# Cluster attention and two mixers on one core: the set-up of the first two head pairs in another order

## The chip, the cores and the metric

The kernel runs on one core of one Trainium2 chip. The metric is the device time of one execution in microseconds; lower is better. Engines: PE (TensorE, matmuls and transposes), PEld (its weight loads), DVE (VectorE), ACT (ScalarE), POOL (GpSimd) and SP (SyncE, which here only issues DMAs). Every time in this document is in microseconds unless it says otherwise.

## The reference

Attention over clusters: every query and key row is assigned to the nearest of 16 centroids of its head, and a query sees only the keys with its own assignment. Two mixers follow.

```python
batch, n_heads, seq, head_dim = (2, 8, 768, 64)   # 16 centroids per head
q_assign = np.argmax(np.einsum('bhsd,hcd->bhsc', q_n, c_n), axis=-1)
k_assign = np.argmax(np.einsum('bhsd,hcd->bhsc', k_n, c_n), axis=-1)
mask = q_assign[:, :, :, None] == k_assign[:, :, None, :]
scores = np.where(mask, scale * np.matmul(q, k.transpose(0, 1, 3, 2)), -1000000000.0)
...
x = np.matmul(attn, v)          # softmax of scores; then heads joined to 512 columns
u = x + (xt @ U @ V).transpose(0, 2, 1)
x = u + np.maximum(u @ w_ch1, 0.0) @ w_ch2
u = x + (np.maximum(xt @ w_tok1, 0.0) @ w_tok2).transpose(0, 2, 1)
return u + np.maximum(u @ w_ch1, 0.0) @ w_ch2
```

The weights, U and V arrive as 64-bit floats and are converted to 32 bits inside the kernel.

## The kernel before

The order of work is written out by hand; the framework only adds the waits. Two heads make a pair, and there are eight pairs. The attention of a pair is twelve tiles of 128 queries by 768 keys, so 96 tiles in all, n = 0 to 95 (the "thirteenth tile" has n = 12).

A matrix product of 32-bit precision is made of operands split into a rounded high part and the rest (low part). For each pair and each of its two halves `a` (one head each) a query stack `qS` and a key stack `kS` hold high and low parts in 128 partitions, with 16 rows of the cluster mask in between; there are two sets of stacks, used in turn by even and odd pairs. Rows of the other half come by copies from SBUF to SBUF (`cross`, two DMAs of 32 partitions each).

The work around the change:

- **Set-up of pair 0** (`setup`): the centroids are loaded (issued at 0.72) and q and k of the pair (k issued at 1.17), stacks are cleared, the centroids are normalised on DVE and transposed on PE into `zc`. For each half ACT rounds q and k (L435, L436), POOL takes the low part of k (L437), DVE that of q (L438). Then the argmax: `scores` (eight small matmuls), `scores_out` (DVE transpose out of PSUM), `arg0` to `arg4` and `mask_rows`, after which eight small DMAs bring the mask rows into the stacks (`stack(0, a, "mask", ...)`, half of them issued by ACT, half by SP).
- **Pair 1 in the set-up**: `load_pair(1)` on SP, ACT rounds (`q_hi`, `k_hi`), SP copies the high parts into set 1 (`stack(1, a, "hi", sp)`, eight DMAs), and `scores(1)`, `scores_out`, `q_lo`, `k_lo` and the copies of the low parts (six DMAs) stand behind the first two tiles' score matmuls `s_mm` and maxima `s_max`. One half of the high copies has 384 + 192 + 2 x 96 KB, one of the low copies 192 + 2 x 96 KB: 2304 KB in all.
- **Tiles**: `step(n)` issues tile n's transposes `t_mm` (six), the score matmuls and maximum of tile n + 2, the exponential `s_exp` of tile n + 1 on ACT, the copies `t_out` of the transposes out of PSUM, and from tile 6 on the products with v (`pv`). The score matmuls of tile n + 2 write the banks that the exponential of tile n reads. Lists attach other work to a tile: `mid` and `low` (PE), `acts` (ACT, ahead of the exponential) and `late` (at the end).
- In those lists: pair 1's argmax on tiles 0 to 5 and its mask DMAs on 6; `load_pair(2)` on 1; `load_uv` (three copies of V and one of U, 192 KB each) on 3; the load of v for pair 1 on 4; pair 2's scores on 9, its `q_hi` on 7 and `k_hi` on 9; U's first conversion step (ACT, L96) on 11.

Later pairs are prepared like pair 2, a few tiles ahead of their own.

Of the kernel before, what the change touches and what calls it, by code (L numbers as in the profile page):

```python
# [10 lines left out]
F32R = mybir.dt.float32r  # L11
# [4 lines left out]
ALU = mybir.AluOpType  # L16
AX = mybir.AxisListType

P = 128
# [5 lines left out]
def tile_cluster_attention__then__two_mixers(  # L25
# [58 lines left out]
    def sub(eng, o, a, b):  # L84
        eng.tensor_tensor(out=o, in0=a, in1=b, op=ALU.subtract)  # L85
# [93 lines left out]
    def load_pair(g, eng=sp):  # L179
        b, p = divmod(g, NPAIR)  # L180
        eng.dma_start(Rq, qT[b, p])
        eng.dma_start(Rk, kT[b, p])
# [7 lines left out]
    def scores(g):  # L190
        p = g % NPAIR
        held["sc"] = bk = ring()
        for qd in range(4):
            src = (Rq, Rk)[qd // 2]
            mm(ps[32 * qd : 32 * qd + 32, bk, 0:HS], zc[:, ts(p, 32)], src[:, ts(qd % 2, HS)], True, True)

    def scores_out():
        dve.transpose(out=am1, in_=ps[:, held["sc"], 0:HS])
# [32 lines left out]
    def mask_rows(eng):  # L231
        eng.tensor_scalar(out=om, in0=ohT, scalar1=msk[:, 0:1], scalar2=msk[:, 1:2], op0=ALU.add, op1=ALU.mult)

    def q_hi():
        rnd(act, Hq.bitcast(F32R), Rq, 0.125)

    def k_hi():
        rnd(act, Hk.bitcast(F32R), Rk)

    def q_lo(eng, o):  # L240
        eng.scalar_tensor_tensor(out=o.bitcast(F32R), in0=Rq, scalar=0.125, in1=Hq, op0=ALU.mult, op1=ALU.subtract)

    def k_lo(eng, o):
        sub(eng, o.bitcast(F32R), Rk, Hk)
# [5 lines left out]
    def cross(o, src, a, eng):  # L250
        m, x, _ = rows(a)
        for i in range(2):
            eng.dma_start(o[x, 1 - i, :], src[m.start + 32 * i : m.start + 32 * i + 32])

    def stack(g, a, what, eng, Lq=Rq, Lk=Rk):
        q, k = f32(qS[g % NST][a]), f32(kS[g % NST][a])
        m, _, y = rows(a)
        if what == "hi":
            eng.dma_start(q[m, :, :], Hq[m].unsqueeze(1).to_broadcast([64, 2, S]))
            eng.dma_start(k[m, 1, :], Hk[m])  # L260
            cross(k, Hk, a, eng)
        elif what == "lo":
            eng.dma_start(k[m, 0, :], Lk[m])
            cross(q, Lq, a, eng)
        else:
            e = eng if type(eng) is tuple else (eng, eng)
            for h in range(2):
                e[h].dma_start(q[y, 0, ts(h, HS)], om[32 * h + 16 * a : 32 * h + 16 * a + 16])
                e[1 - h].dma_start(k[y, 0, ts(h, HS)], om[64 + 32 * h + 16 * a : 80 + 32 * h + 16 * a])
# [113 lines left out]
        return [lambda: rnd(act, uh, o), lambda: sub(dve, ul, o, f32(uh))]  # L383


    def setup():
        with tc.tile_pool(name="tmp", bufs=1) as tmp:
            cc = tmp.tile([P, 2, D], F32, name="cc")
            tiny = tmp.tile([P, 1], F32, name="tiny")
            act.dma_start(cc[:, 0, :], cen)  # L390
            sp.dma_start(cc[:, 1, :], cen)
            sp.dma_start(Rq, qT[0, 0])
            act.dma_start(Rk, kT[0, 0])
            load_v(0)
            make_identity(nc, ident)
            dve.memset(zc, 0.0)
            for t in (qS, kS):
                for i in range(NST):
                    (dve, pool)[i].memset(f32(t[i][1])[32:64], 0.0)
            wi = tmp.tile([P, 16], F32, name="wi")  # L400
            pool.iota(wi, pattern=[[-1, 16]], base=16, channel_multiplier=0, allow_small_or_imprecise_dtypes=True)
            dve.memset(msk[0:64, 0:1], 0.0)
            dve.memset(msk[0:64, 1:2], 1.0)
            dve.memset(msk[64:128, 0:1], -1.0)
            dve.memset(msk[64:128, 1:2], BIG)


            sq = tmp.tile([P, D], F32, name="sq")
            n2 = tmp.tile([P, 1], F32, name="n2")
            n1 = tmp.tile([P, 1], F32, name="n1")  # L410
            nr = tmp.tile([P, 1], F32, name="nr")
            dve.tensor_tensor(out=sq, in0=cc[:, 0, :], in1=cc[:, 0, :], op=ALU.mult)
            dve.tensor_reduce(out=n2, in_=sq, axis=AX.X, op=ALU.add)
            dve.tensor_scalar(out=n2, in0=n2, scalar1=2.0 ** -100, scalar2=None, op0=ALU.max)
            act.activation(n1, n2, AF.Sqrt)
            dve.reciprocal(nr, n1)
            dve.tensor_tensor(out=nr, in0=nr, in1=n2, op=ALU.mult)
            dve.tensor_tensor(out=n1, in0=n1, in1=nr, op=ALU.add)
            dve.tensor_scalar(out=n1, in0=n1, scalar1=0.5, scalar2=1e-6, op0=ALU.mult, op1=ALU.add)
            dve.reciprocal(nr, n1)  # L420
            dve.tensor_scalar(out=cc, in0=cc, scalar1=nr, scalar2=None, op0=ALU.mult)
            ct = ps[:, 6, 0:P]
            pe.transpose(ct, cc.rearrange("p a d -> p (a d)"), ident)
            for a in range(2):
                dve.tensor_copy(
                    zc[64 * a : 64 * a + 64, :].rearrange("p (h j) -> p h j", j=32)[:, :, 16 * a : 16 * a + 16],
                    ct[64 * a : 64 * a + 64].rearrange("p (h j) -> p h j", j=32)[:, :, 16 * a : 16 * a + 16],
                )
            dve.tensor_copy(wcl, wi)

            l = p32[0]
            for a in range(2):
                m, _, _ = rows(a)
                q, k = qS[0][a], kS[0][a]
                rnd(act, q[m], Rq[m].unsqueeze(1).to_broadcast([64, 2, S]), 0.125)  # L435
                rnd(act, k[m, 1, :], Rk[m])  # L436
                sub(pool, k[m, 0, :], Rk[m], f32(k[m, 1, :]))  # L437
                dve.scalar_tensor_tensor(out=l[m].bitcast(F32R), in0=Rq[m], scalar=0.125, in1=f32(q[m, 0, :]), op0=ALU.mult, op1=ALU.subtract)  # L438
                cross(f32(k), f32(k[:, 1, :]), a, (act, sp)[a])
                cross(f32(q), l, a, sp)  # L440
            act.activation(tiny, n1, AF.Exp, scale=0.0)
            scores(0)
            scores_out()
            load_pair(1)
            arg0()
            arg1(dve)
            arg2()
            arg3(dve)
            arg4()
            mask_rows(dve)  # L450
            for a in range(2):
                stack(0, a, "mask", (act, sp))
            q_hi()
            k_hi()
            for a in range(2):
                stack(1, a, "hi", sp)
            s_mm(0)
            s_mm(1)
            s_max(0)
            s_max(1)  # L460
            scores(1)
            scores_out()
            q_lo(dve, Rq)
            k_lo(pool, Rk)
            for a in range(2):
                stack(1, a, "lo", sp)


    x_ = xn[:, 1].rearrange("p a b c -> p (a b c)")
# [97 lines left out]
    def at(d, s, f):  # L567
        d.setdefault(max(s, 0), []).append(f)

    for g in range(G):  # L570
        s0 = NTT * g
        for h in range(2):
            s = s0 + 2 * NT * h + 4 * NT + 1
            at(mid, s, lambda q=2 * g + h: merge(q))
            at(late, s, lambda q=2 * g + h: merge_out(q))
        n, s1 = g + 1, s0
        if 2 <= n < G:
            at(late, s1 - 8 if n > 2 else 1, lambda g=n: load_pair(g))
            at(low, s1 - 3, lambda g=n: scores(g))
            at(acts, s1 - 5, q_hi)  # L580
            at(acts, s1 - 3, k_hi)
            for s, f in ((-3, scores_out), (-2, arg0), (-1, lambda: q_lo(dve, Rq)),
                         (-1, lambda: arg1(pool)), (-1, lambda: k_lo(pool, Rk)), (3, arg2), (3, lambda: arg3(pool)),
                         (5, arg4), (5, lambda: mask_rows(pool))):
                at(late, s1 + s, f)
            for what, s in (("hi", -2), ("lo", 1), ("mask", 7)):
                for a in range(2):
                    at(late, s1 + s, lambda g=n, a=a, w=what: stack(g, a, w, sp))
        if n < G:
            at(late, s1 + 6 if n > 1 else 4, lambda g=n: load_v(g))  # L590
# [6 lines left out]
    for t in range(NS):  # L597
# [5 lines left out]

        at(mid, s, za)
        at(late, s if s == 69 else s + 1, lambda t=t: zadd_out(0, t, held["za"]))
    for s, f in ((0, arg0), (1, lambda: arg1(pool)), (2, arg2), (3, lambda: arg3(pool)), (4, arg4), (5, lambda: mask_rows(pool))):
        at(late, s, f)
    for a in range(2):
        at(late, 6, lambda a=a: stack(1, a, "mask", sp))
    at(late, 3, load_uv)  # L610
    for i, s0, ss in ((0, 11, (12, 12, 12, 12)), (1, 13, (14, 16, 18, 20))):
        at(acts, s0, uv[i][0])
        for f, s in zip(uv[i][1:], ss):
# [360 lines left out]
```

## Time and profile before

| | us |
|---|---|
| median of 3 runs | 767.53 (767.29 to 768.66) |
| the profiled execution | 767.95 |
| its span (first to last instruction) | 766.2 |
| PE busy | 738.7 (96%) |
| DVE busy | 467.1 (61%) |
| ACT busy | 310.1 (40%) |
| POOL busy | 166.4 (22%) |

The share of an engine is an average over stages with different limits. The 1.75 us between the profiled execution's time and its span lie ahead of the first and behind the last instruction. Times in the rows of the trace count from the start of the span.

### The profile page before, as it was taken

The numbers are of one execution on the slowest core, as the hardware profiler recorded it, in microseconds if no ns is written. First come the engines' busy times: TensorE is split into PE (matmuls) and PEld (weight loads), VectorE is DVE, ScalarE is ACT, GpSimd is POOL, SyncE is SP. The second block draws the span as 40 slices with busy tenths as digits, with TensorE's granted clock in tenths as the row PEclk, the third lists the DMA queues.
The fourth block names the chain that finished last, engine by engine and source line by source line (L and its number), as shares of the span: only waits on it lengthen the run. The fifth ranks groups of instructions, "written<-read, shape, count | busy, mean of one in ns | idle before, by whom it ended". The sixth has DMA issues, their size and how long they took to land.

```text
span 766.2 us, 10466 instructions
## 1 busy us (share of the span) xinstructions
PE 738.7 (96%) x3845; PEld 582.1 (76%) x3845; DVE 467.1 (61%) x689; ACT 310.1 (40%) x565; POOL 166.4 (22%) x147
## 2 busy tenths in 40 slices
PE   1899999999999999999999999999999999999998
PEld 0667766766666688888888888888888888888886
DVE  6778988877777366875758587666675432122113
ACT  3777877867776343332232324323232311111010
POOL 3321432421310122321322122125211410000000
PEclk9999999999999999999999999999999999999999
DMA  5886777875311344753632699967885647555652
GB/s 152 191 185 185 179 186 188 243 183 134 87 63 55 112 165 151 287 193 138 220 131 89 222 346 368 337 238 259 283 286 215 214 144 274 192 192 195 243 192 83
DMA packets 51714, 149.38 MB, mean 195 GB/s; under 512 B 7792, under 2 KB 15984, under 8 KB 49616
## 3 DMA queue, kind: packets, MB, share of 16 engines
q1 hardware_dynamic: 51152, 148.01, 59.7%
q10 hardware_dynamic: 512, 0.72, 0.3%
q8 instruction: 30, 0.49, 0.3%
q14 instruction: 20, 0.16, 0.1%
HBM read 97.32 MB, written 32.51 MB: 169 GB/s over the span
## 4 chain that ended last, share of the span: by engine, by line
PE 92%; DVE 3%; DMA 2%; ACT 2%; issue 1%; SPq 0%; ACTq 0%; DVEq 0%
PE ps L73 82%; PE ps L314 7%; DVE nm L292 1%; DMA xn<-in_U_dram 1%; ACT p L297 1%; ACT qk L78 1%; PE ps L377 1%; PE ps L822 1%; PE ps L334 1%; DMA sq__81<-in_qT_dram 1%; DMA qk<-om 0%; SPq L476 0%; DVE u_sb L100 0%; DVE xn L373 0%; DVE qk L85 0%
## 5 line engine op out<-in xcount | busy, mean ns | idle before, releaser
L727 DVE SCALAR_TENSOR_TENSOR gl<-ps,gh 128x512 fp32r<-128x512 f32 x84 | 58.0, 691 | 209.6 <-ACT gh L726 209.6
L73 PE MATMUL ps<-gh,qk 128*128 128x512 f32 x544 | 179.6, 391 | 0.1
L726 ACT ACTIVATE gh<-ps 128x512 fp32r<-128x512 f32 x84 | 50.2, 598 | 312.9 <-PE ps L73 311.5
L73 PE MATMUL ps<-qk 112*128 112x384 f32 (+2 forms) x456 | 110.8, 370 | 13.0 <-DMA qk<-om 10.3
L73 PEld LDWEIGHTS ps<-gh,qk 128*128 128x128 f32 x544 | 102.1, 188 | 21.6 <-issue 0.5
L292 DVE TENSOR_REDUCE nm<-ps 128x1 f32<-128x768 f32 x96 | 91.8, 956 | 41.5 <-PE ps L73 38.8
L73 PEld LDWEIGHTS ps<-qk 112*128 112x128 f32 (+1 forms) x456 | 77.2, 192 | 44.5 <-issue 20.7
L73 PE MATMUL ps<-gl,qk 128*128 128x512 f32 x272 | 106.1, 390 | 0.0
L85 POOL TENSOR_TENSOR qk<-c__77,qk 128x512 fp32r<-128x512 f32 x40 | 54.9, 1381 | 197.0 <-ACT qk L78 169.1
L297 ACT ACTIVATE p<-ps,nm 128x768 f32<-128x768 f32 x96 | 86.6, 902 | 7.4 <-DVE nm L292 6.8
L314 PE MATMUL ps<-ident,p 128*128 128x128 f32 x576 | 82.1, 275 | 2.6 <-DVE z L360 0.6
L314 PEld LDWEIGHTS ps<-ident,p 128*128 128x128 f32 x576 | 67.6, 140 | 12.8 <-ACT p L297 2.6
L73 PE MATMUL ps<-u2h,qk 128*128 128x512 f32 x224 | 73.9, 391 | 0.0
L73 PE MATMUL ps<-pt,vr 128*64 128x384 f32 x384 | 72.1, 498 | 0.0
L321 ACT COPY pt<-ps 128x512 f32<-128x512 f32 x96 | 56.1, 584 | 35.1 <-PE ps L314 34.7
L73 PEld LDWEIGHTS ps<-gl,qk 128*128 128x128 f32 x272 | 51.1, 188 | 10.2
L73 PE MATMUL ps<-u1h,qk 128*128 128x512 f32 x160 | 52.6, 390 | 0.0
L100 DVE TENSOR_SCALAR c__77<-c__77 128x512 f32<-128x512 f32 (+2 forms) x47 | 49.1, 1045 | 0.8 <-ACT c__77 L96 0.7
L73 PEld LDWEIGHTS ps<-u2h,qk 128*128 128x128 f32 x224 | 42.1, 188 | 8.6
L109 DVE SCALAR_TENSOR_TENSOR c__77<-c__76,c__77 128x512 int32<-128x512 int32 (+2 forms) x47 | 43.4, 923 | 1.5
L106 DVE SCALAR_TENSOR_TENSOR c__77<-c__76,c__77 128x512 int32<-128x512 int32 (+2 forms) x47 | 43.5, 925 | 1.1
L73 PE MATMUL ps<-u2l,qk 128*128 128x512 f32 x112 | 43.6, 390 | 0.0
(146 smaller groups left out, 1017.0 us busy)
## 6 DMA issues: line engine op xcount, KB each, us to landing
qk<-scr_b SPq DMA_DIRECT2D x72, 512.0 KB, 4.2
c__76<-in_wa_dram SPq DMA_DIRECT2D x16, 1024.0 KB, 4.8
qk<-scr_a SPq DMA_DIRECT2D x32, 512.0 KB, 7.6
c__76<-in_wb_dram SPq DMA_DIRECT2D x24, 512.0 KB, 5.1
scr_b<-qk SPq DMA_DIRECT2D x24, 512.0 KB, 4.2
scr_a<-wx SPq DMA_DIRECT2D x16, 512.0 KB, 2.9
scr_a<-qk SPq DMA_DIRECT2D x16, 512.0 KB, 2.7
qk<-sq__81 SPq DMA_DIRECT2D x14, 384.0 KB, 4.0
```

The lines of the kernel that those rows point to most:

```text
L73: pe.matmul(o, lhsT=l, rhs=r, start=start, stop=stop, **kw)
L78: act.activation(o, i, AF.Copy, scale=scale)
L85: eng.tensor_tensor(out=o, in0=a, in1=b, op=ALU.subtract)
L100: dve.tensor_scalar(out=dst, in0=dst, scalar1=2.0 ** -15, scalar2=122879.9921875, op0=ALU.max, op1=ALU.min)
L106: dve.scalar_tensor_tensor(out=d, in0=lo, scalar=29, in1=d, op0=ALU.logical_shift_right, op1=ALU.bitwise_or)
L109: dve.scalar_tensor_tensor(out=d, in0=hi, scalar=-0x40000000, in1=d, op0=ALU.bitwise_and, op1=ALU.bitwise_or)
L292: dve.tensor_reduce(out=nm[:, n % 4 : n % 4 + 1], in_=ps[:, b0 : b0 + 2, 0:HS], axis=AX.XY, op=ALU.max, negate=True)
L297: act.activation(p32[n % NP32].rearrange("p (j k) -> p j k", j=2), ps[:, b0 : b0 + 2, 0:HS], AF.Exp, bias=nm[:, n % 4 : n % 4 + 1], accum_ ...
L314: pe.transpose(ps[:, tb[j], ts(i, P)], p32[n % NP32][:, ts(c, P)], ident)
L321: act.copy(o, ps[:, tb[j], :])
L726: act.activation(gh, o, AF.Relu)
L727: dve.scalar_tensor_tensor(out=gl, in0=o, scalar=0.0, in1=f32(gh), op0=ALU.max, op1=ALU.subtract)
```

## The change

In the set-up, all four clearings of stacks go to POOL. Pair 0's argmax scores are issued after its first half's roundings; the low parts of both halves are taken in two small functions, `low_q` and `low_k`: the first half's ahead of the argmax (DVE and POOL), the second half's behind it (both on DVE). The key copies of the first half are issued by SP and those of the second by ACT (it was the other way round). PE is given 48 transposes of the identity into a bank that nobody reads, ahead of the first tile's matmuls. Pair 1 leaves the set-up but for its load, which GpSimd's queue issues behind the second half's low parts. Its scores, rounding (k on POOL), low parts, argmax and copies are attached to tiles 1 to 6; two steps of its argmax (`arg3`, `mask_rows`) go from POOL to DVE. `load_pair(2)` goes from tile 1 to 4, pair 2's `q_hi` from tile 7 to 9, and `load_uv` from tile 3 to the end of tile 6.

```diff
--- before.py
+++ after.py
@@ -383,6 +383,8 @@
         return [lambda: rnd(act, uh, o), lambda: sub(dve, ul, o, f32(uh))]
 
 
+    WARM = 48
+
     def setup():
         with tc.tile_pool(name="tmp", bufs=1) as tmp:
             cc = tmp.tile([P, 2, D], F32, name="cc")
@@ -394,9 +396,9 @@
             load_v(0)
             make_identity(nc, ident)
             dve.memset(zc, 0.0)
-            for t in (qS, kS):
-                for i in range(NST):
-                    (dve, pool)[i].memset(f32(t[i][1])[32:64], 0.0)
+            for i in range(NST):
+                for t in (qS, kS):
+                    pool.memset(f32(t[i][1])[32:64], 0.0)
             wi = tmp.tile([P, 16], F32, name="wi")
             pool.iota(wi, pattern=[[-1, 16]], base=16, channel_multiplier=0, allow_small_or_imprecise_dtypes=True)
             dve.memset(msk[0:64, 0:1], 0.0)
@@ -428,20 +430,31 @@
                 )
             dve.tensor_copy(wcl, wi)
 
-            l = p32[0]
+            l = p32[3]
+
+            def low_q(a):
+                m, _, _ = rows(a)
+                dve.scalar_tensor_tensor(out=l[m].bitcast(F32R), in0=Rq[m], scalar=0.125, in1=f32(qS[0][a][m, 0, :]), op0=ALU.mult, op1=ALU.subtract)
+                cross(f32(qS[0][a]), l, a, sp)
+
+            def low_k(a, eng):
+                m, _, _ = rows(a)
+                sub(eng, kS[0][a][m, 0, :], Rk[m], f32(kS[0][a][m, 1, :]))
+
             for a in range(2):
                 m, _, _ = rows(a)
                 q, k = qS[0][a], kS[0][a]
                 rnd(act, q[m], Rq[m].unsqueeze(1).to_broadcast([64, 2, S]), 0.125)
                 rnd(act, k[m, 1, :], Rk[m])
-                sub(pool, k[m, 0, :], Rk[m], f32(k[m, 1, :]))
-                dve.scalar_tensor_tensor(out=l[m].bitcast(F32R), in0=Rq[m], scalar=0.125, in1=f32(q[m, 0, :]), op0=ALU.mult, op1=ALU.subtract)
-                cross(f32(k), f32(k[:, 1, :]), a, (act, sp)[a])
-                cross(f32(q), l, a, sp)
+                cross(f32(k), f32(k[:, 1, :]), a, (sp, act)[a])
+                if a == 0:
+                    scores(0)
+            low_q(0)
+            low_k(0, pool)
             act.activation(tiny, n1, AF.Exp, scale=0.0)
-            scores(0)
             scores_out()
-            load_pair(1)
+            for i in range(WARM):
+                pe.transpose(ps[:, 5, ts(i % 4, P)], ident, ident)
             arg0()
             arg1(dve)
             arg2()
@@ -450,20 +463,13 @@
             mask_rows(dve)
             for a in range(2):
                 stack(0, a, "mask", (act, sp))
-            q_hi()
-            k_hi()
-            for a in range(2):
-                stack(1, a, "hi", sp)
+            low_q(1)
+            low_k(1, dve)
+            load_pair(1, pool)
             s_mm(0)
             s_mm(1)
             s_max(0)
             s_max(1)
-            scores(1)
-            scores_out()
-            q_lo(dve, Rq)
-            k_lo(pool, Rk)
-            for a in range(2):
-                stack(1, a, "lo", sp)
 
 
     x_ = xn[:, 1].rearrange("p a b c -> p (a b c)")
@@ -575,9 +581,9 @@
             at(late, s, lambda q=2 * g + h: merge_out(q))
         n, s1 = g + 1, s0
         if 2 <= n < G:
-            at(late, s1 - 8 if n > 2 else 1, lambda g=n: load_pair(g))
+            at(late, s1 - 8 if n > 2 else 4, lambda g=n: load_pair(g))
             at(low, s1 - 3, lambda g=n: scores(g))
-            at(acts, s1 - 5, q_hi)
+            at(acts, s1 - 5 if n > 2 else 9, q_hi)
             at(acts, s1 - 3, k_hi)
             for s, f in ((-3, scores_out), (-2, arg0), (-1, lambda: q_lo(dve, Rq)),
                          (-1, lambda: arg1(pool)), (-1, lambda: k_lo(pool, Rk)), (3, arg2), (3, lambda: arg3(pool)),
@@ -603,11 +609,14 @@
 
         at(mid, s, za)
         at(late, s if s == 69 else s + 1, lambda t=t: zadd_out(0, t, held["za"]))
-    for s, f in ((0, arg0), (1, lambda: arg1(pool)), (2, arg2), (3, lambda: arg3(pool)), (4, arg4), (5, lambda: mask_rows(pool))):
+    at(low, 1, lambda: scores(1))
+    for s, f in ((1, scores_out), (1, q_hi), (1, lambda: rnd(pool, Hk.bitcast(F32R), Rk)), (2, lambda: k_lo(pool, Rk)), (2, arg0),
+                 (2, lambda: arg1(pool)), (3, lambda: q_lo(dve, Rq)), (5, arg2), (5, lambda: arg3(dve)), (6, arg4), (6, lambda: mask_rows(dve))):
         at(late, s, f)
-    for a in range(2):
-        at(late, 6, lambda a=a: stack(1, a, "mask", sp))
-    at(late, 3, load_uv)
+    for what, s in (("hi", 2), ("lo", 3), ("mask", 6)):
+        for a in range(2):
+            at(late, s, lambda a=a, w=what: stack(1, a, w, sp))
+    at(late, 6, load_uv)
     for i, s0, ss in ((0, 11, (12, 12, 12, 12)), (1, 13, (14, 16, 18, 20))):
         at(acts, s0, uv[i][0])
         for f, s in zip(uv[i][1:], ss):
```

## Rows read from the trace of the kernel before

**Rows 1.** Waits of PE from 45 to 766: total, times, longest.

```profile
PE ps L377 <- DVE xn L342: 0.7, 1, 0.7
```

**Rows 2.** Timeline from 31.8 to 62: start, duration, engine, line, operation, [idle before].

```profile
45.53 0.95 PE L73 MATMUL ps<-qk 112*128 112x384 f32 x4 [0.55 <-DMA qk<-om]
...
47.44 0.38 ACT L96 ACTIVATE u_sb<-xn 128x192 f32<-128x192 f32 x1
...
47.73 0.88 ACT L297 ACTIVATE p<-ps,nm 128x768 f32<-128x768 f32 x1
...
49.89 0.98 PE L73 MATMUL ps<-qk 112*128 112x384 f32 x4
```

**Rows 3.** Timeline from 0 to 32, PE.

```profile
7.83 0.85 PE L73 MATMUL ps<-sq__81,zc 128*32 128x384 f32 x2 [0.55 <-DVE zc L425]
...
19.03 2.90 PE L73 MATMUL ps<-qk 112*128 112x384 f32 x8 [9.70 <-DMA qk<-om]
...
23.98 1.04 PE L314 MATMUL ps<-ident,p 128*128 128x128 f32 x8
...
28.12 0.98 PE L73 MATMUL ps<-qk 128*128 128x384 f32 x4 [1.98 <-ACT p L297]
```

**Rows 4.** Timeline from 0 to 32, DVE, ACT and POOL.

```profile
1.34 1.34 DVE L399 MEMSET qk<- 32x1536 f32 x1 [0.35 <-issue]
...
4.53 0.23 DVE L412 TENSOR_TENSOR sq<-cc 128x64 f32<-128x64 f32 x1
...
5.86 1.48 ACT L78 ACTIVATE qk<-sq__81 64x1536 fp32r<-64x1536 f32 x1 [0.42 <-DMA sq__81<-in_qT_dram]
...
8.16 2.34 POOL L85 TENSOR_TENSOR qk<-sk__82,qk 64x768 fp32r<-64x768 f32 x1 [3.90 <-ACT qk L78]
...
10.91 0.95 DVE L438 SCALAR_TENSOR_TENSOR p<-sq__81,qk 64x768 fp32r<-64x768 f32 x1 [2.08 <-ACT qk L78]
11.63 1.28 ACT L441 ACT_TABLE_LOAD   x1
...
11.90 0.58 DVE L198 STREAM_TRANSPOSE am<-ps 128x384 f32<-128x384 f32 x1
...
13.10 0.87 DVE L215 TENSOR_TENSOR am<-am,amx 128x384 bf16<-128x384 f32 x1
...
16.19 0.48 DVE L232 TENSOR_SCALAR om<-ohT,msk 128x384 f32<-128x384 bf16 x1
...
26.10 0.94 DVE L292 TENSOR_REDUCE nm<-ps 128x1 f32<-128x768 f32 x1
...
27.08 0.90 ACT L297 ACTIVATE p<-ps,nm 128x768 f32<-128x768 f32 x1 [1.88 <-DVE nm L292]
```

**Rows 5.** Chain of waits from 14 to 60: start, duration, what.

```profile
37.16 6.62 DMA xn<-in_U_dram
...
43.80 1.75 DMA qk<-om
```

**Rows 6.** DMA issues around 1, 14.78 and 34.21: KB, time to landing.

```profile
...
sk__82<-in_kT_dram ACTq DMA_DIRECT2D x1, 384.0 KB, 4.9
...
cc<-in_cen_dram ACTq DMA_DIRECT2D x1, 32.0 KB, 1.9
...
sk__82<-in_kT_dram SPq DMA_DIRECT2D x1, 384.0 KB, 3.6
...
sk__82<-in_kT_dram SPq DMA_DIRECT2D x1, 384.0 KB, 5.8
```

**Rows 7.** Timeline of SP's queue from 20 to 35.

```profile
20.32 0.70 SPq L259 DMA_DIRECT2D qk<-sq__81  x1
...
30.54 1.23 SPq L253 DMA_DIRECT2D qk<-sq__81  x2
33.71 0.33 SPq L181 DMA_DIRECT2D sq__81<-in_qT_dram  x1
...
34.60 1.60 SPq L476 DMA_DIRECT2D xn<-in_V_dram  x1
```

## The prediction

> **What bounds the kernel now.** I read the profile from the back to the front. The list of what PE waited for from 45 us to the end has six entries of one wait each, the longest 0.7 us, 3.0 us in all [rows 1]. So from about 45 us PE sets the end, and a change in the set-up is worth exactly what it moves the moment from which PE runs without a break. As the mark I take the fifteenth tile's score matmuls, now at 49.89 [rows 2]: from there on both programs issue the same PE work. What must be found is when the mark comes after the change.
>
> Before it PE starves twice. The first tile matmul starts at 19.03, after 9.7 us of waiting for the mask rows [rows 3]. The timeline shows what these waited for: DVE's subtraction for the second half (10.91) stands in front of the argmax, which runs from 11.90 to 16.67 [rows 4]. The second place is tile 12's matmuls at 45.53, released by a mask DMA [rows 2]; the chain of waits leads from it to the DMA of U, issued at 37.16 and landed at 43.78, with the mask DMA issued at 43.80 [rows 5]. I read from this that a DMA of SP is issued only when the one eight issues earlier has landed.
>
> **The change, part by part.**
>
> *Memsets.* Two of 1.34 us leave DVE [rows 4]. POOL does all four, from 1.35 to about 6.7, while it has nothing else until 8.16, so they cost nothing; without that cover they would hold POOL's subtraction. DVE's centroid arithmetic starts at 4.53 now [rows 4]; its data were issued at 0.72 and took 1.9 [rows 6], so it can start 1.9 sooner, and the argmax scores, now at 7.83 [rows 3], would be ready at 5.9. They then wait for k, issued at 1.17 and 4.9 in flight [rows 6]: 6.1. Two rounds of at most 0.85 end by 7.8.
>
> *The argmax first.* ACT has q's first half rounded at 5.86 + 1.48 = 7.34; DVE's first subtraction (0.95, as its twin) ends at 8.3 and the argmax follows at once, 3.6 us before its old 11.90. Its instructions took 16.67 - 11.90 = 4.77 [rows 4]. POOL's subtraction runs beside it to about 10.5 as now (8.16 + 2.34) and could hold the comparison (L215), due at 9.5, by up to 1.0; but L215 took 0.87 even now, longer than the steps around it, so something of that is in the 4.77 already, and I take nothing more. Mask rows: 13.1. ACT issues half of their DMAs; it runs its old instructions in another order, so it is through its table load at 11.63 + 1.28 = 12.9 [rows 4], just in time. The old 19.03 - 16.67 = 2.36 from rows to matmul [rows 3, 4] gives the first tile matmul at 15.45.
>
> *Unread transposes.* Rows show two paces of PE, though the clock column prints 1.00 throughout: eight score matmuls took 2.90 at 19.03 after 9.7 us without work, four took 0.98 at 28.12 after 1.98 us without [rows 3]; I read them as the 1.2 and the 2.4 GHz level. Eight transposes took 1.04 at 23.98 [rows 3]: at most 0.13 each at the fast pace, so 0.11 with the last one's tail taken off, and twice that, 0.22, at the slow. Forty-eight from 7.8 on end at 13.1 (all fast) or 18.4 (all slow). They are over by 15.45 if no more than 21 are slow. I take fewer, since by 23.98 PE was fast after 5 us of work, some of which was itself fast; then they cost nothing, and the first four matmuls take 0.98 instead of half of 2.90, 0.5 less. The first exponential starts at 15.45 + 0.98 + 0.94 for the maximum [rows 4]: 17.4.
>
> *Second pair by GpSimd's queue.* The load now waits for DVE's last two subtractions: 13.1 + 2 x 0.95 = 15.0. No DMA of GpSimd's queue is in this trace. By the nearest rows, k took 3.6 in the set-up and 5.8 later through SP [rows 6]; so it lands between 18.6 and 20.8. I take the middle, since both ends are the same transfer under different load. Its first readers are the scores in tile 1: exponentials at 17.4 and 18.4, the next matmuls 1.04 after the second (as 27.08 to 28.12 [rows 3, 4]), 0.98 for them and six transposes: 21.1; and ACT's rounding of q, behind the third exponential (20.4 to 21.3) and one copy out of PSUM (0.58, as L198): 21.9 to 22.8, priced as an exponential of the same shape, 0.90. So the load is hidden, with 0.3 to 2.5 to spare; a gain below nothing is excluded, since nothing reads it sooner. POOL's new rounding of k, priced as the nearest POOL row, 2.34 [rows 4], ends by 23.2. The Trainium skill (DMA: Bandwidth & Descriptors, Specifications) gives the GpSimd path about 1 us to the first byte and the others about 0.6; by that estimate the landing comes 0.4 later and is still hidden; no row here shows it.
>
> *The pair's copies on SP.* Fourteen DMAs, 2.3 MB by the code, are issued from 20.32 to 31.77 [rows 7], 0.2 MB a microsecond, back to back; that 11.45 stays. They start when q is rounded, at 22.8 and not 20.32: done 34.3. The third pair's load, now moved to tile 4, comes, as before, when the copies have landed, 33.71 - 20.32 = 13.4 after the first [rows 7] (the load of v fits in between): q at 36.2, k 0.5 later, landing 3.6 later [rows 6] at 40.3. Tile 9's scores read it; PE wants them at about 39, a new wait of 1.3. Eight mask DMAs follow on SP; the eighth waits for k, so it leaves SP at about 40.9. Then V, V, V and U, moved from tile 3 to behind the masks in tile 6. From the first V to U's landing it was 43.78 - 34.60 = 9.2 [rows 5, 7], with the 0.77 MB of q and k ahead of them; at 0.2 MB a microsecond that is 3.7, so 5.5 are left and U lands at 46.5. Bounds: 44.7, if only its and V's 0.77 MB count (3.8), and 50.1, if all 9.2 stay. I take 5.5 because q and k have landed by then.
>
> *The mark.* ACT's first step on U (0.38) stands in tile 11 ahead of the thirteenth exponential [rows 2]. Now U has been there for 3.7 us; after the change ACT waits for it: exponential at 46.9 (47.73 now), the mark 1.04 later: 47.95 instead of 49.89 [rows 2]. The 3.6 us won at the first tile, 4.1 with the faster matmuls, shrink to 1.9. Such a sum assumes that every other engine follows at once; DVE takes two argmax steps over from POOL in tiles 5 and 6 (about 1.0), and I leave 0.1 for it: 1.8. The profiled execution took 767.95, so 766.15; the median of the runs is 0.42 lower: 765.7.
>
> **Rivals.**
>
> *U is in time.* If V and U need only the 3.8, ACT waits no more than PE does. Then k is the last thing late: 40.3, rounding 0.90, an exponential to the next matmuls 1.04: tile 12's matmuls at 42.3 instead of 45.53, 3.2 won, 764.3. For it: their rings are empty by then. Against: U alone was 6.6 in flight [rows 5].
>
> *The gain is eaten at U.* If the third pair's k takes its present 5.8 instead of 3.6 [rows 6], mask, V and U come 2.2 later: mark at 50.15, 0.3 lost, 767.8: no change. For it: v's load now goes ahead of it. Against: V no longer runs beside it. A GpSimd load that lands after about 21.5 does the same, microsecond for microsecond.
>
> *The transposes hold PE, and slowly* (the other side). If all 48 run at 0.22, PE is at them until 18.4, the first tile comes 2.95 later and its matmuls at the slow pace another 0.5; everything up to U's landing follows: mark at 51.4, 1.5 lost, 769.0. It decides from the 22nd slow transpose. For it: no stretch of the trace has transposes alone, and matmuls after long idleness are slow. Against: at 23.98 eight transposes were fast, though right behind matmuls. The Trainium skill (TensorE: Matmul & The Clock Gate, Part 4: PE-mode transpose) says that transposes do not count as PE work in the way that raises the clock; by that rule this rival holds with its 769.0, and no row here refutes it.
>
> **How the numbers follow.** Forecast 0.48, U in time 0.12, gain eaten 0.20, slow transposes 0.20. The time is the forecast's, 765.7. On this kernel 0.2% is 1.5 us, about what a measurement can tell from no change. The forecast's own spread is 0.9 either way (k 0.7, U 0.6), so 0.33 of its 0.48 lies beyond 1.5; with U in time 0.45 is faster. Of the slow transposes 0.12, and 0.05 from U's far bound, are slower; 0.38 remain. The range runs from U in time to the slow transposes, 764.4 to 769.0; the forecast alone has 764.8 to 766.6.
>
> **What would show it.** The argmax from 8.3 to 13.1; first tile matmul at 15.45, its four within 1.0; transposes first 0.22 and then 0.11 apart, over by 15.4; GpSimd's loads landed by 20.8; first copy of the pair issued at 22.8; the third pair's k landed at 40.3; U landed at 46.5 and ACT waiting for it; the mark at 48.0. It is wrong if PE is still at transposes when the mask rows land, if tile 1's scores wait for GpSimd's load, if ACT finds U there, or if the copies take another time than 11.45.

## The result and the profile after

The changed kernel takes 771.72 us (median of 6 runs, 769.75 to 772.73) against 767.35 (766.90 to 768.66) for the kernel before, measured beside it: ratio 1.0052, 95% interval [1.0038, 1.0066]. It is slower by 4.4 us, where 1.8 faster was forecast, and outside the predicted range. The profiled execution took 772.73, the slowest of the six, with a span of 770.9 (766.2 before). Compared instruction by instruction on PE, it is 3.99 later at the mark (53.88 against 49.89) and 3.54 later at tile 18 (tiles are numbered from 0); it loses 0.4 near 260 us and 0.5 in small steps near 225 and 708; PE ends 4.49 later. So the start decides, as assumed, but with the other sign. The gain of the first tiles is real and lasts until tile 11, whose matmuls start 2.92 sooner than before (38.46 against 41.38); it is lost at tiles 12 to 14, which start 1.47, 2.90 and 3.99 later than before.

The timeline of PE after the change (columns as in [rows 2]):

```profile
7.98 7.17 PE L457 MATMUL ps<-ident 128*128 128x128 f32 x48
15.55 1.80 PE L73 MATMUL ps<-qk 112*128 112x384 f32 x8 [0.40 <-DMA qk<-om]
18.72 1.65 PE L73 MATMUL ps<-qk 112*128 112x384 f32 x4 [1.38 <-ACT p L297]
20.17 1.91 PE L314 MATMUL ps<-ident,p 128*128 128x128 f32 x8
21.90 1.62 PE L73 MATMUL ps<-qk 128*128 128x384 f32 x4
23.32 1.05 PE L314 MATMUL ps<-ident,p 128*128 128x128 f32 x4
...
38.46 0.95 PE L73 MATMUL ps<-qk 128*128 128x384 f32 x4
...
43.00 0.84 PE L73 MATMUL ps<-sq__81,zc 128*32 128x384 f32 x4 [1.70 <-DMA sq__81<-in_qT_dram]
45.01 0.89 PE L73 MATMUL ps<-sk__82,zc 128*32 128x384 f32 x4 [1.17 <-DMA sk__82<-in_kT_dram]
47.00 1.65 PE L73 MATMUL ps<-qk 112*128 112x384 f32 x4 [1.11 <-ACT p L297]
48.44 1.91 PE L314 MATMUL ps<-ident,p 128*128 128x128 f32 x8
50.01 1.63 PE L73 MATMUL ps<-qk 112*128 112x384 f32 x4
...
53.88 0.99 PE L73 MATMUL ps<-qk 112*128 112x384 f32 x4
```

The same tile 11 before:

```profile
41.38 0.94 PE L73 MATMUL ps<-qk 128*128 128x384 f32 x4
```

The first tile matmul comes at 15.55, 3.48 sooner than in [rows 3], and at the fast pace: eight in 1.80, where four took 0.98 and eight slow ones 2.90. The transposes are over at 15.15. Then four matmuls take 1.65 again, at 18.72 and at 47.00. The view of the busy time by stretch says why (start:end and length of the stretch, busy time of PE, PEld, DVE, ACT and POOL with the number of their instructions, granted clock of PE, share of the DMA engines, GB/s):

```profile
11.50:18.30 6.80, 5.45 (x41) 4.72 (x39) 5.07 (x8) 2.11 (x3) 1.30 (x2) 1.00 0.56 133
18.40:25.20 6.80, 6.48 (x28) 5.07 (x28) 2.62 (x4) 3.43 (x9) 0.83 (x1) 0.50 0.28 78
25.20:45.60 20.40, 16.64 (x108) 11.99 (x104) 13.76 (x19) 12.29 (x24) 4.81 (x4) 1.00 0.79 182
45.70:52.50 6.80, 5.69 (x24) 4.98 (x24) 2.76 (x4) 4.48 (x10) 2.08 (x3) 0.50 0.92 218
```

The granted clock is 0.50, the 1.2 GHz level, in two stretches, 18.4 to 25.2 and 45.7 to 52.5; they are called the first and the second dip below. The first begins at 18.36, inside the wait of 1.38 us ahead of 18.72. The second begins at 45.67, after waits of 1.70 and 1.17 us for the third pair's q and k; another of 1.11, for an exponential, follows ahead of 47.00. The profile of the kernel before has no such stretch: its first record of the clock is 1.0 at 22.97, and it stays there until the end of the work.

The dips are not the whole loss. Of the six runs of the changed kernel, the one with a mean granted clock of 1.000 took 769.75, still 2.4 more than the kernel before; the other five, at 0.990 to 0.996, took 771.00 to 772.73.

What PE and ACT waited for shows in the DMA issues between 13 and 52 (columns: KB of one, median us from issue to landing), and in the timelines of SP and ACT:

```profile
sq__81<-in_qT_dram POOLq DMA_DIRECT2D x1, 384.0 KB, 4.4
sk__82<-in_kT_dram POOLq DMA_DIRECT2D x1, 384.0 KB, 5.7
...
sk__82<-in_kT_dram SPq DMA_DIRECT2D x1, 384.0 KB, 5.3
...
qk<-p SPq DMA_DIRECT2D x2, 96.0 KB, 5.5
xn<-in_U_dram SPq DMA_DIRECT2D x1, 192.0 KB, 4.0
```

```profile
15.78 1.17 SPq L253 DMA_DIRECT2D qk<-p  x2
25.77 0.70 SPq L259 DMA_DIRECT2D qk<-sq__81  x1
...
39.26 0.35 SPq L181 DMA_DIRECT2D sq__81<-in_qT_dram  x1
39.71 0.37 SPq L182 DMA_DIRECT2D sk__82<-in_kT_dram  x1
...
44.98 0.51 SPq L269 DMA_DIRECT2D qk<-om  x1
45.53 1.52 SPq L482 DMA_DIRECT2D xn<-in_V_dram  x3
47.09 0.42 SPq L483 DMA_DIRECT2D xn<-in_U_dram  x1
```

```profile
24.41 0.59 ACT L321 COPY pt<-ps 128x512 f32<-128x512 f32 x1 [1.66 <-PE ps L314]
24.89 0.85 ACT L78 ACTIVATE sq__81<-sq__81 128x768 fp32r<-128x768 f32 x1
...
42.93 0.84 ACT L78 ACTIVATE sq__81<-sq__81 128x768 fp32r<-128x768 f32 x1 [4.04 <-DMA sq__81<-in_qT_dram]
...
51.12 0.39 ACT L96 ACTIVATE u_sb<-xn 128x192 f32<-128x192 f32 x1 [1.00 <-DMA xn<-in_U_dram]
51.41 0.88 ACT L297 ACTIVATE p<-ps,nm 128x768 f32<-128x768 f32 x1
```

They are to be read as one chain. The second pair's q is rounded at 24.89, behind a copy out of PSUM that waited for PE's transposes. The first copy of the pair follows at 25.77 (20.32 before, [rows 7]), and the third pair's load leaves 13.5 after it, at 39.26 (33.71 before). Its k lands at 39.71 + 5.25 = 44.96; the last mask DMA (44.98, eight issues behind that k), V (45.53) and U (47.09, landed 51.10) come behind it, and ACT waits 1.00 for U ahead of the exponential at 51.41. The mark is 2.47 behind that exponential; PE is at the low clock until 52.49 and comes to it late (1.02 behind it in e1, which has no second dip).

### The profile page after: what moved, and what is told of

Same layout as the page of the kernel before. It is cut to its first block, busy times and chain, and to the rows that moved or that the text cites. A ratio compares the mean times of both kernels' runs of the same rounds, so it can differ in the third digit from the quotient of the medians.

```text
span 770.9 us, 10567 instructions
## 1 busy us (share of the span) xinstructions
PE 750.2 (97%) x3893; PEld 592.4 (77%) x3893; DVE 464.2 (60%) x690; ACT 310.4 (40%) x564; POOL 167.2 (22%) x148
## 4 chain that ended last, share of the span: by engine, by line
PE 92%; DVE 3%; DMA 2%; ACT 2%; issue 1%; SPq 0%; DVEq 0%; ACTq 0%
PE ps L73 82%; PE ps L314 8%; DVE nm L292 1%; ACT p L297 1%; DMA qk<-om 1%; PE ps L377 1%; PE ps L334 1%; PE ps L831 1%; DMA sq__81<-in_qT_dram 1%; DMA qk<-scr_b 1%; ACT qk L78 1%; DVE xn L373 0%; DVE qk L85 0%; DVE amx L206 0%; DVE p L437 0%
## 5 line engine op out<-in xcount | busy, mean ns | idle before, releaser
L73 PE MATMUL ps<-qk 112*128 112x384 f32 (+2 forms) x456 | 112.4, 374 | 4.2 <-ACT p L297 3.2
L73 PEld LDWEIGHTS ps<-qk 112*128 112x128 f32 (+1 forms) x456 | 78.0, 194 | 35.1 <-ACT p L297 13.4
L314 PE MATMUL ps<-ident,p 128*128 128x128 f32 x576 | 84.0, 281 | 2.3 <-DVE z L360 0.6
L314 PEld LDWEIGHTS ps<-ident,p 128*128 128x128 f32 x576 | 70.0, 144 | 11.7 <-ACT p L297 2.4
L73 PEld LDWEIGHTS ps<-pt,vr 128*64 128x64 f32 x384 | 23.4, 136 | 26.5 <-issue 26.5
```

The source lines that it names most:

```text
L73: pe.matmul(o, lhsT=l, rhs=r, start=start, stop=stop, **kw)
L314: pe.transpose(ps[:, tb[j], ts(i, P)], p32[n % NP32][:, ts(c, P)], ident)
```

## The experiments

The theory after this result: the tiles from 12 on are set by a chain of one pair's load, its rounding, its 2.3 MB of copies, the next pair's load, and so on; the change starts that chain later by 5.4 us (first copy 25.77 against 20.32), and each wait of PE can bring the low clock on top. The rivals: GpSimd's queue alone, the unread transposes, U alone, or the argmax's new order. The mark is tile 14. The table has the times of one profile of each kernel, and the medians of its runs (us; the mark and tile 24 as differences from before's 49.89 and 73.85; the ratio is to the kernel before, measured beside it):

| kernel | first copy | third pair's k landed | U landed | mark | tile 24 | median | ratio, 95% interval |
|---|---|---|---|---|---|---|---|
| before | 20.32 | 40.04 | 43.78 | | | 767.35 | |
| after | 25.77 | 44.96 | 51.10 | +3.99 | +3.54 | 771.72 | 1.0052 [1.0038, 1.0066] |
| e1 | 25.92 | 44.88 | 50.94 | +2.38 | +2.86 | 770.48 | 1.0030 [1.0012, 1.0047] |
| e2 | 24.37 | 43.28 | 50.44 | +2.23 | +1.79 | 770.56 | 1.0026 [1.0012, 1.0041] |
| e3 | 25.22 | 44.39 | 50.53 | +2.73 | +3.39 | 771.83 | 1.0050 [1.0035, 1.0065] |
| e5 | 22.50 | 41.98 | 48.06 | -0.49 | -0.15 | 769.08 | 1.0015 [1.0000, 1.0029] |
| e6 | 22.83 | 41.95 | 48.90 | +0.33 | +0.09 | 769.05 | 1.0016 [1.0003, 1.0030] |
| e8 | 21.50 | 41.23 | 47.99 | -2.27 | +3.69 | 770.77 | 1.0035 [1.0016, 1.0054] |
| e9 | 21.52 | 40.36 | 48.09 | -3.12 | -1.06 | 768.51 | 1.0013 [0.9991, 1.0035] |
| e10 | 20.90 | 38.93 | 42.40 | -0.21 | -0.22 | 768.99 | 1.0018 [1.0009, 1.0027] |
| e11 | 21.14 | 40.79 | 49.85 | -2.70 | -2.62 | 765.19 | 0.9965 [0.9952, 0.9978] |
| e12 | 24.50 | 43.37 | 50.22 | +2.01 | +1.56 | 771.20 | 1.0037 [1.0024, 1.0050] |
| e4 | 24.57 | 43.06 | 49.80 | +1.18 | +1.18 | 770.95 | 1.0039 [1.0024, 1.0053] |

A profile is one execution, and the low clock comes in some executions of a kernel and not in others (above: 0.990 to 1.000 in runs of the changed kernel); so the place of a wait is read from the profile, and the price of a kernel from its median.

**e1: the second pair's load on SP.**

```diff
-            load_pair(1, pool)
+            load_pair(1)
```

> The changed kernel with pair 1 loaded by SP's queue at the same place of the program instead of by GpSimd's. Theory P (PE's slow stretch from 18.4 to 25.2 sets the time of q's rounding, and the copies on SP, the third pair's load and U follow it): the load lands up to 2 us sooner, but tile 1's scores and q's rounding still come at 24.3 to 24.9; the first copy of the pair stays within 0.5 us of 25.8 and the time within 0.5 us of the changed kernel's. Theory L (the GpSimd load, landed at 21.45, is the delay): the copies start 1.5 to 3 us sooner and the time falls by as much.

The load is issued 2.5 later (17.38) and lands in 3.3 and 3.5 at 20.66 and 21.61, no sooner than GpSimd's. The clock is at 0.5 from 18.62 to 25.45 all the same, and the first copy stays at 25.92. GpSimd's queue is not the cause by itself. The median falls by 1.2, more than the 0.5 expected: in this profile the clock doesn't fall a second time. U lands only 0.16 sooner than in the changed kernel (50.94), but the mark comes 1.02 behind the exponential instead of 2.47, and 1.60 sooner.

**e2: the clock kept up.** Twelve more unread transposes stand between the first two tiles' matmuls and the third's.

```diff
             s_mm(1)
+            for i in range(12):
+                pe.transpose(ps[:, 5, ts(i % 4, P)], ident, ident)
             s_max(0)
```

> The changed kernel with 12 more unread transposes behind the first two tiles' score matmuls, so that PE works through its idle time from 17.35 to 18.7. Theory P: if PE keeps the fast pace in tiles 0 and 1, q is rounded at about 22 and the copies start at 22.8 to 23.5 instead of 25.8, the third pair's k lands 2.5 to 3 us sooner, and the time falls by 2.5 to 4.5 us, back to that of the kernel before or a little under it. If the clock falls all the same, nothing changes and this run says nothing. Theory L: the copies start at 25 or later, less than 1 us won. Theory O (the order alone: pair 1's load and copies now start behind the argmax, whatever PE's pace): under 1 us.

The clock is 1.0 from 9.61 on, past the place of the first dip, and the first copy moves from 25.77 to 24.37: the first dip costs 1.4. The clock falls at 43.74 instead, after waits of 2.29 and 0.52 for the third pair's q and k. The first copy doesn't reach 22.8, so something else holds it, and the median falls by 1.2 and not by the 2.5 to 4.5 expected.

**e6: both together**, the lines of e1 and e2.

> The changed kernel with both: pair 1 loaded by SP's queue, and 12 more unread transposes behind the first two tiles' score matmuls. Each alone left the copies of pair 1 at 25.9 and 24.4. Theory R (two causes stand in parallel at tile 3: PE's slow pace, and the second half's q copies, which land at 21.2 to 21.7 because 768 KB of GpSimd's load go ahead of them in the rings): with both away tile 3's matmuls come at about 20.3 instead of 21.6 to 21.9, but k of pair 1 lands at 21.6, so the scores of tile 1 wait for it; copies start at 23.0 to 23.7, the mark (tile 14) at 51 to 52, the time 1 to 2 us under that of the changed kernel with the transposes alone. Theory P alone: nothing beyond what the transposes gave, copies at 24.4.

Now the first copy is at 22.83. The timeline of PE, and the DMA issues of the copies between the two halves:

```profile
18.45 0.98 PE L73 MATMUL ps<-qk 112*128 112x384 f32 x4
19.26 1.04 PE L314 MATMUL ps<-ident,p 128*128 128x128 f32 x8
20.05 0.95 PE L73 MATMUL ps<-qk 128*128 128x384 f32 x4
...
qk<-p SPq DMA_DIRECT2D x2, 96.0 KB, 2.2
```

The fourth tile's matmuls start at 20.05 instead of 21.90. They read the two 96 KB copies that cross q's low parts between halves (qk<-p). Behind GpSimd's 768 KB these were 5.5 in flight; ahead of the load, on SP, 2.2. In e12, whose front part is that of the changed kernel but whose profile has no dip there, PE names them:

```profile
18.43 0.98 PE L73 MATMUL ps<-qk 112*128 112x384 f32 x4 [1.37 <-ACT p L297]
19.25 1.04 PE L314 MATMUL ps<-ident,p 128*128 128x128 f32 x8
21.73 0.94 PE L73 MATMUL ps<-qk 128*128 128x384 f32 x4 [1.45 <-DMA qk<-p]
```

So either one alone hides the other: at the low clock the copies are in time, and at the high clock PE waits for them. Taken out together they are worth 2.94 at the first copy (1.40 and nothing alone). The median, 769.05, is 1.5 below e2's, as expected. What is left of e6's loss stands on ACT (timeline of e6): U is late by 3.06, and the mark is 1.02 behind the exponential.

```profile
48.92 0.37 ACT L96 ACTIVATE u_sb<-xn 128x192 f32<-128x192 f32 x1 [3.06 <-DMA xn<-in_U_dram]
49.20 0.88 ACT L297 ACTIVATE p<-ps,nm 128x768 f32<-128x768 f32 x1
```

**e3: no unread transposes.**

```diff
-    WARM = 48
+    WARM = 0
```

> The changed kernel without its 48 unread transposes. Theory P, as the rows of the kernel before read: PE starts its first tile at the slow pace at 15.5, is slow for the first two tiles as well, and the copies start within 1 us of 25.8; the time stays within 1 us of the changed kernel's, so the transposes bought nothing. Rival: the transposes are what made the clock fall at 18.4 (they were read as no work), and without them the clock rises at about 20 and the time falls by 2 us or more.

771.83 against 771.72: the 48 transposes neither gain nor cost anything that can be measured. They do bring the high clock sooner (first record 1.0 at 11.54; without them at 23.06) and make the first eight matmuls faster (1.80 against 2.90), but the tile after them starts only 0.21 sooner (18.72 against 18.93).

**e5: the second pair's roundings one tile sooner.**

```diff
-    for s, f in ((1, scores_out), (1, q_hi), (1, lambda: rnd(pool, Hk.bitcast(F32R), Rk)), (2, lambda: k_lo(pool, Rk)), (2, arg0),
+    for s, f in ((1, scores_out), (0, q_hi), (0, lambda: rnd(pool, Hk.bitcast(F32R), Rk)), (2, lambda: k_lo(pool, Rk)), (2, arg0),
-    for what, s in (("hi", 2), ("lo", 3), ("mask", 6)):
+    for what, s in (("hi", 1), ("lo", 3), ("mask", 6)):
```

> The changed kernel with q's and k's rounding of pair 1 attached to tile 0 instead of 1 and the high copies to tile 1 instead of 2; everything else is left. Theory C (the start of the copies on SP carries everything behind it): the first copy starts at about 22.0 to 22.6 instead of 25.8, all fourteen are out 3.2 to 3.8 us sooner, the third pair's k lands by as much sooner and the mark (tile 14's score matmuls, 53.88) comes 3 to 4 us sooner; time 767.5 to 768.5. Theory O2 (tiles 0 to 2 are late anyway, because PE is slow until 25.2): the copies start sooner, but tiles 3 to 8 keep their times and the mark moves by less than 1.5 us.

The first copy comes 3.27 sooner, U lands 3.04 sooner, and the mark is 4.48 sooner than in the changed kernel: 3.0 through U, the rest because the clock doesn't fall a second time. So the later start of the chain is the cause of most of the loss at the mark. The median falls by less than expected, to 769.08; a part of that in this profile is a wait of 1.6 for the DMA of a converted weight block (qk<-scr_b) near the end, which was 0.2 in the changed kernel's.

**e8 and e9: as e5, and U needed later; e9 with e2's transposes too.**

```diff
-    for i, s0, ss in ((0, 11, (12, 12, 12, 12)), (1, 13, (14, 16, 18, 20))):
+    for i, s0, ss in ((0, 15, (16, 16, 16, 16)), (1, 13, (14, 16, 18, 20))):
```

> Rounding and copies of pair 1 one tile sooner (as in the run before it), and U's conversion in tiles 15 and 16 instead of 11 and 12. With the rounding sooner alone, tile 12's matmuls came at 44.0, U landed at 48.06 and tile 14's matmuls at 49.40. Theory U (the wait for U is what stands between the two): tile 14 at 46.6 to 47.3, which is 2.6 to 3.2 before the kernel before; time 764.6 to 766. Rival (tile 14 is set by the maxima and by PE's products with v, not by U): tile 14 at 48.5 or later, under 1 us won.

> As the run before it with 12 more unread transposes behind the first two tiles' score matmuls. Theory R: rounding of q at 20.5 instead of 21.6, copies start at about 21.4, the third pair's k lands 1 us sooner, tile 14 about 1 us sooner than without them, 45.6 to 46.3; time 763.6 to 765. Rival (k's landing at 21.2 and its rounding by POOL at 22.0 hold the second copy, so the copies end when they did): within 0.4 us of the run without them.

The mark is 2.27 and 3.12 sooner than before the change: here the forecast's gain is, and more. But the medians, 770.77 and 768.51, lie far above the expected 764.6 to 766 and 763.6 to 765: the gain is lost again at tile 22. (The first copy comes at 21.52 in e9 and at 21.50 in e8, whose profile has no first dip even without the transposes.) In e9 ACT's list of waits from 60 to 70, and the DMA issues from 58 to 72, show the next link of the same chain, the fourth pair's load (read by the rounding of its q):

```profile
ACT sq__81 L78 <- DMA sq__81<-in_qT_dram: 3.5, 1, 3.5
```

```profile
sq__81<-in_qT_dram SPq DMA_DIRECT2D x1, 384.0 KB, 3.4
sk__82<-in_kT_dram SPq DMA_DIRECT2D x1, 384.0 KB, 4.6
```

That load is issued at 62.46, hardly sooner than before (63.41), while the tiles come 3 us sooner. In e8 ACT waits 5.2 and PE 4.1 there, and the clock falls during PE's wait (the row of 68.2 to 74.9, columns as above); tile 24 is 3.69 late:

```profile
68.20:74.90 6.70, 4.72 (x18) 4.53 (x19) 1.82 (x2) 5.28 (x10) 0.00 (x0) 0.50 0.44 119
```

Runs of one kernel spread accordingly: e8's from 766.43 to 772.73, e9's from 765.58 to 772.24.

**e10: the argmax's new order alone.** Set-up and lists treat the second pair as before; clearings, order of the argmax and transposes are the change's, and the load is SP's, behind the mask rows.

```diff
-            load_pair(1, pool)
+            load_pair(1)
+            q_hi()
+            k_hi()
+            for a in range(2):
+                stack(1, a, "hi", sp)
...
-            at(late, s1 - 8 if n > 2 else 4, lambda g=n: load_pair(g))
+            at(late, s1 - 8 if n > 2 else 1, lambda g=n: load_pair(g))
...
-    at(late, 6, load_uv)
+    at(late, 3, load_uv)
```

> The first half of the change alone: the argmax first, the clearings on POOL and the 48 transposes; pair 1 is loaded by SP behind the second half's low parts and otherwise prepared in the set-up as before, and the tile lists are those of before. Theory C (the chain of pair 1's load and copies sets tile 12, not the argmax): the load is issued 0.5 to 2 us later than before, the copies start at 21 to 22.5 (20.32 before), and the time is 0 to 1.5 us above the kernel before although the first tile starts 3.5 us sooner. Rival (the loss is all in moving pair 1 into the tiles): the 3.5 us of the first tile are kept at least in part, time 1 to 3 us under the kernel before.

```profile
15.29 1.66 PE L73 MATMUL ps<-qk 112*128 112x384 f32 x8
20.05 1.50 PE L73 MATMUL ps<-sq__81,zc 128*32 128x384 f32 x4 [3.10 <-DMA sq__81<-in_qT_dram]
21.04 1.49 PE L73 MATMUL ps<-sk__82,zc 128*32 128x384 f32 x4
22.80 1.65 PE L73 MATMUL ps<-qk 112*128 112x384 f32 x4 [0.26 <-ACT p L297]
```

The first tile comes 3.73 sooner than before and the third only 0.37: the second pair's load is issued 2.5 later than before (16.67 against 14.15), and PE waits 3.10 for it. Here a first tile that comes sooner is worth nothing, because the load behind it doesn't come sooner too. The median is 0.2% above before's, as Theory C expected; in this profile the mark is 0.21 sooner than before, and the loss of 1.1 stands near 708, at a wait for a converted weight block.

**e11, e12, e4: the fourth pair's load made sooner.** The 1 MB load of the first wide weight block stands on SP at tile 8, ahead of the third pair's copies, and is first read in tile 23. e11 is e9 with that load at tile 18; e12 is the changed kernel with this alone.

```diff
-    early = [(8, 0, 1), (23, 0, 3), (24, 0, 4), (28, 0, 4.5), (30, 0, 5), (32, 0, 5.5), (35, 0, 6), (36, 0, 6.5), (40, 0, 7),
+    early = [(18, 0, 1), (23, 0, 3), (24, 0, 4), (28, 0, 4.5), (30, 0, 5), (32, 0, 5.5), (35, 0, 6), (36, 0, 6.5), (40, 0, 7),
```

> The kernel of e9 (second pair's rounding and copies sooner, transposes kept up to the first tile, first step on U at tile 15) with the 1 MB load of the first wide weight block issued at tile 18 instead of tile 8. Theory: what took e9's 3.1 us away at tile 22 (the fourth pair's q rounding waited 3.5 us for its load) is the volume in the rings ahead of that load, so with 1 MB taken out of 44 to 60 us the load lands about 3 us sooner, tile 24 starts at 70.2 to 71.2 (73.85 before, 72.79 in e9), and the time falls to 764 to 765.5. Rival: the load is held by the third pair's own copies and waits, and not by the volume; tile 24 stays at 72.5 to 73 and the time at 768 to 769.

> The changed kernel with only the 1 MB load of the first wide weight block moved from tile 8 to tile 18. Theory: it stands on SP behind U, so up to the mark nothing moves by more than 1 us (mark at 52.9 to 53.9), and what is left behind the mark is PE alone: 770.8 to 772. Rival: the volume of that load is what makes U late: U lands 2 us or more sooner, mark at 52 or below, 769.5 or less.

e11 takes 765.19, ratio 0.9965 [0.9952, 0.9978]: faster than both kernels. The fourth pair's q is issued at 58.87 (62.46 in e9) and lands at 61.91 (65.86). So the expected 3 us are there, but nearly all of them (3.6 of 3.95) are an earlier issue, and only 0.4 a shorter flight: what the 1 MB load held up was SP's queue more than the transfer. PE's list of waits from 60 to 766 has no entry over 1.1, and the granted clock is 1.00 from 10.27 to the end:

```profile
PE ps L377 <- DVE xn L342: 1.1, 1, 1.1
PE ps L314 <- DVE z L360: 0.6, 1, 0.6
PE ps L73 <- DMA qk<-om: 0.5, 1, 0.5
```

```profile
10.00:20.00 10.00, 9.33 (x72) 8.57 (x70) 6.90 (x11) 3.57 (x7) 1.30 (x2) 1.00 0.61 156
20.00:60.00 40.00, 35.97 (x233) 26.09 (x233) 29.23 (x45) 29.59 (x58) 12.66 (x11) 1.00 0.78 175
```

In e12 the same move is worth nothing that can be told (1.0037 against 1.0052, intervals overlapping): with e11 this says that the link that it loosens binds only once the ones ahead of it are loose. Its mark, 51.90, lies below what I expected because its profile lacks the first dip, not because of U, which landed at 50.22 (50.44 in e2, which lacks that dip too and has the 1 MB load at tile 8).

**e4: U needed later, alone** (e8's line in the changed kernel).

> The changed kernel with only the first steps on U moved from tiles 11 and 12 to tiles 15 and 16. Theory that the copies of the second pair and the third pair's load set the tiles and U adds its 1.0 us wait at most: mark at 52.5 to 53.2, 770.5 to 771.5. Rival, that U is what the whole loss hangs on: mark at 50 or below, 768 or less.

770.95 us, as expected of a wait of 1.0 at most; the mark of 51.07 is again that of a profile without the first dip. U alone is not the cause.

## Why the prediction was wrong

**Right.** The argmax ran from 8.48 to 13.24 (8.3 to 13.1 predicted), the first tile at 15.55 (15.45), its matmuls at the fast pace, the transposes over at 15.15, 17 of them slow (0.21 apart) where 21 were the limit. The copies took 11.5 (11.45), the third pair's load left 13.5 behind the first of them (13.4), U landed 5.57 after the first V was issued (5.5), and ACT waited for it. These intervals came as forecast; the chain that carries them started late. Two smaller slips cost nothing: the argmax scores came at 6.54 and not 6.1, and the 0.77 MB that the sum takes at 3.7 is 3.85 at its own 0.2 MB a microsecond.

**The step that failed: "They start when q is rounded, at 22.8".** The first copy came at 25.77, 2.97 later. On the way to that rounding the sum had PE at the fast pace throughout, and no wait for the copies that cross q's low parts. Two things were missing. PE's clock fell at 18.36, inside the third tile's wait of 1.38; the sum let such a gap cost nothing, as [rows 3] has it, where matmuls stay fast after 1.98 without work. And it priced GpSimd's load by what waits for it, not by what is in flight beside it: the crossing copies of q, which the fourth tile's matmuls read, went from 2.2 to 5.5 in flight. With both taken out (e6) the step gives 22.83, and by the forecast's path: rounding at 21.96 (21.9). The prediction had said that a load landing after 21.5 would delay the chain; it landed at 21.45, and did its harm to another transfer.

**A term mis-sized: k's flight.** 5.25 instead of 3.6, 1.65 more; this is what the second rival feared. What sets it stays open: it was 4.3 to 5.3 in the kernels that have the change's lists, and 5.83 before against 3.84 in e10, where the loads around it are issued in the same order.

**A term missing: the exponential to the mark.** 1.04 was taken and 2.47 measured: PE had waited for the third pair's load, a wait that the prediction named (1.3) without a cost at the clock, and the clock fell at 45.67. In e6 and e1, without the second dip, it is 1.02. The three make 2.97 + 1.65 + 1.43 = 6.05; with 0.1 won back on the rest of the way, that is the mark's error of 5.93.

**The rivals.** None gave this time. The gain was eaten at U and by k as the second rival says, but that rival lost 2.2 in all, through k alone; here k lost 1.65, and the later start and the second dip the rest. The rule of the Trainium skill (TensorE: Matmul & The Clock Gate, Part 4: PE-mode transpose) behind the third rival does not hold for the transposes here: the trace's clock record turns to 1.0 at 11.54, when PE had done nothing but transposes since its last score matmul ended at 8.05, and they go from 0.21 to 0.11 apart; without them (e3) that record comes at 23.06. What was not among the cases is a chain that begins later and a clock that falls at the waits it makes.

**Left open.** The 0.4 near 260 us (a wait of 1.1 instead of 0.7 for DVE's xn, in every kernel whose second pair is prepared in the tiles, not in e10), and what PE loses near 708 to 712, 0 to 1.9 in the profiles (a wait for a converted weight block, of at most 1.6), with no order that the runs show. The change's parts that lie between pair 1 and U (the third pair's load from tile 1 to 4, V and U from tile 3 to behind the masks) were not undone one by one; only U's first use was moved.

## What to carry to other kernels

Winning time at the first tile paid here only where the next stage's load was issued sooner as well; follow the transfers link by link (load, rounding, copies, next load) and ask of each what it is behind. When a transfer moves to another queue, price the small transfers that land behind it, not only its own readers. And a wait of PE of one or two microseconds may cost as much again at the low clock (up to 1.4 at the two places here), in some executions and not in others, so a version is compared by its median and explained by the profile.

## What was unexpected of the hardware

The same wait can be followed by the low clock or not: 1.38 us ahead of the third tile's matmuls in the changed kernel was followed by 0.50 for 6.8 us, 1.37 at the same place in e12 by none, and 1.98 in [rows 3] by none.

Two 96 KB copies inside SBUF, on SP's queue, took 5.5 us beside 768 KB whose loads GpSimd's queue issued within a microsecond of them, and 2.2 when the same 768 KB came later on SP. GpSimd's own transfers of 384 KB took 4.4 and 5.7, where SP's in e1 took 3.3 and 3.5.

POOL rounded 128x768 in 0.83 (its subtraction of 64x768 in [rows 4] took 2.34, and 2.34 was taken).
